# Attention into an MoE layer: exponentials summed as a tree with adding DMAs, one matmul per bias sum, joined halves of w_out, and a new order

## The chip, the cores and the metric

One core of a Trainium2 chip. The metric is the device time of one execution in microseconds (us). Before the change: median 605.57 us of 3 runs (604.0 to 606.81).

## The reference

Inputs: q, k, v with 4 batches, 12 heads, 448 rows, 64 per head; w_in (768 x 2048) and w_out (2048 x 768), which come as float64; scalars cap, s, b.

```python
scores = scale * np.matmul(q, k.transpose(0, 1, 3, 2))
scores = cap * np.tanh(scores / cap)
attn = np.exp(scores - max)
attn = attn / (np.sum(attn, axis=-1, keepdims=True) + 1e-09)
x = np.matmul(attn, v)                # to (1792, 768)
h = x @ w_in
g = s * np.maximum(h, 0.0) ** 2 + b
out = (g @ w_out).astype(np.float32)
```

## The kernel before, in words

**Precision.** The two products of the MoE layer run in float16 with every operand split in a high and a low half (hi, lo), so a product is three matmuls. The scales that this needs are found in the kernel. Batches 2 and 3 (and the second product of batch 1) use a scheme with seven products of half size in place of eight; its mixed weights are made in the kernel (`mixq`, `mix`), saved to DRAM and loaded again.

**Attention (`scores`, `pvs`).** A pair of heads gives three full tiles of 128 keys and a tail of 64 keys, which two pairs share. TensorE makes the scores in fp32, ScalarE runs tanh and exp (L441, L445) into a tile of 128 x 2 x 448 from the pool "ph" (the tail: "pt"), TensorE multiplies by v (L496, L505). The row sums come from a matmul with ones (`total`, L536). For batches 1 to 3 (`LEVEL` is 3) the tiles of a pair are added up first: three adds into a sum of its own from the pool "acc" (L522): tile 0 plus tile 1, plus tile 2, plus the pair's half (64 rows) of the tail. `binary` (L349 on VectorE, L350 on GpSimd) records them. Then four matmuls make the row sums of two pairs.

**w_out (`piece`, `wout`).** Each sixth d of w_out comes in four quarters q of 128 x 512 float64. Three instructions turn the two 32-bit words of a float64 into one float32: shift the low word (L636, VectorE), scale the high word (L641, ScalarE), and join them (L645, VectorE), which writes into the place of the high words, so that the float32 values lie 8 bytes apart. They are read for the maxima (L739), rounded to float16 in pieces of 256 (`split`: hi on any engine at L341 to L343, lo on VectorE at L360) and summed for the term b times the column sums of w_out, the "bias" (L746: three adds of 512 elements; L752: four fp32 matmuls against a column of ones, one for each block of 128).

**Order.** `Plan` collects operations with their reads and writes. The constant ORDER is a list of their numbers; a suffix a, d or p picks ScalarE, VectorE or GpSimd where an operation has several ways. `emit` issues them in this order, and each engine and DMA queue runs its own in that order. All loads and stores are issued by SP. Each operation of TensorE in the list is a group of matmuls (9 in the seven-product scheme's first product).

**Memory.** One area "bed" is cut into pools; `SLOTS` gives the number of tiles in each: 9 of "w", 5 of "ph", 2 of "acc".

**Lines that the prediction touches:** adds L349 and L350; products L828 to L830, L969, L1056; joins of the seven products L931; bias sum L752; rounding L341, L342; loads of mixed w_in halves L943 (from `wq`).

Of the kernel before, what the change touches and what calls it, by code (L numbers as in the profile page):

```python
# [21 lines left out]
class Plan:  # L22
# [87 lines left out]
FAST = (1, 2, 3)  # L110
LEVEL = (0, 3, 3, 3)
SPLIT = ()
QUICK = (2, 3)
# [7 lines left out]
8 12 10 18 27 795 868 9 4 796 3 13 800 14 19 28 15 63 11 21 16 805 24 858 33 20 22 870 30 17 23 25 802 34 26 67  # L121
35 2 36 29 797 65 5 806 801 811 40 798 847 816 64 799d 807 31 37 859 68 32 852 38 41 79 869 80 69 81 82 42 813
83 871 848 818 808 860 809d 812 821 120 45d 70 863 43 39 88 71 95 803 73 44d 66 804p 56 55 823 814 810 817 861
76 74 72 77 842 862d 822 75 190 819 824 78 815d 85 825d 89 137 820p 54d 826 57 849 853 86 872d 864 90 84 844 118
889 58 189 894 854 91 92 134 60 843 850 59 827 100d 122 96 87 851p 97 46 845 855 865 856d 123 119 47 846d 98 93
828 135 890 866 138 857 124 896 99d 94 829 867d 891 895 125 109d 873 874 128 61p 875 832d 131 136 876 126 102
129 127 101 905 111 0 892 834d 881d 48 882 906 887d 121 110 305 49 193 143 112 885d 140 910 150 897 144 139 132
151 130 888 145 133 899 194 141 113 877d 886 146 195 838d 142 191 147 199 196 878 883d 879d 148 830d 907 912 911
893d 200 941 197 149 201 152 202 833 103 908 913 155d 203 915 898p 205 104 153 208 164d 198 914d 836d 62 204 901
916 839 192 247 211 206 880 209 106 221d 50 214 207 884 215 154d 909d 216 900 902 217 218 105 249 166 210 222d  # L130
903d 917 260 6 212 261 251 252 918 165 156 51 223d 115 107d 167 213 250 157 904 248 919d 254 168 114 253 255
224d 257 258 920 256 921 219 259 220 922 225d 266 923 263 264 226d 272 227 926d 957 229d 169 170 228d 116p 835
262 158 928d 273 927 307 274 318 942 952 267 279d 159 946 275 265 269 319 287d 934d 268 309 161 308 270 171d 310
312 324 280d 831 315 282d 276 943 271 313 316 160 281d 306 283d 320 929 277 278 7 317 284d 162d 944 240 379 314
325 935 285 52d 321 311 326 389 330 936 924d 296d 331 286d 332 381 337p 239 962 289 322 333 338p 108 117 327
238d 948 241 230 242 390 959 163 380 53 383 954 172 323 953 173 244 334 1 439 339d 947 938 945d 328 398 384 340d
937 231 298 288 949 329 399 386 243 335 385 341d 297 387 342d 174 950d 392 336 404 299 175 178d 290 459 939 393
391 382 291 388 958 395 343 405 963 955 176d 396 964 940a 245p 394 397 400 232 437 345d 344d 406 180d 179 411d
401 233 951 407 965 408 402 347 293 495 292 966a 419a 956a 409 960 181 235 177 184d 961d 414d 444 460 182a 1400
967 450 294d 968 403 969 925 185 410 438 445 355 356 447 970 451 441 300 346 186a 187 1448 302 446 354a 412d  # L140
428d 932a 348 973a 452 971a 933 413d 442 1406 497 183 930d 1430 972 496 234 301 448 988 840a 975a 1075 931 443
1401 979d 415d 188 1402 449 1407 1449 1408 983 1403 1431 357 974 976 416d 841 989 1409 1076 980 1450 236d 981d
993 994 984 837 1432 995 998 508 999 1085 977d 509 985 417 990 986 1000 996 505 991 453 456 1001 461 1404a 1087
1003p 440 1090 462 246 982 469d 463 418a 358 421 420 506 1410a 1411p 1092 997 454 992 457 1451 1002 464 349 1412
1413 429 470d 499 514 458 1452d 1478 465 430 1077 1004d 987 1453p 1086 455 431 507 1414 500 1433 589 466 432 467
1078 468 472d 1091 360 1080 502 978 515 603 1008 477a 471d 1009 473d 587 510 503 1010 359 1484 1479 1485 474d
600 1081 1088 1082 1019a 475 1025a 1083 350 1093 1480 1500 1026 1005d 501 504 498 604 520 1095d 1023a 361p 521
1084 1089 295 1481 1021d 303d 601 422 1094 1024 522 1482d 1405d 476a 486a 1415 488 511 434 527d 1015a 517 1016
487 1096p 1006 1454 362 1416d 1017a 351 1013a 1486 605 512 1424 423 433 516 528d 1007 304 352p 1425 1011a 1434a
# [24 lines left out]
1266 1542 760 1690 764p 693 1535 1564p 1258 1530 1276 1267 1268d 1543 1270 1271d 1541 1277 1274 1290 1544 1531
1546d 1052 1592 1567a 1269 1257 1545 1565a 1278 1275 1279 1283 1568d 1566d 1053 1280 1284d 1281d 1547a 1287
1569d 1291 1292 1285 1610 1593 1300 1532 1502 1303 1282 1614 1288 1289 1548d 1293 1570d 1549a 1594 1297 1551d
1571d 1550d 1298d 1572a 1611 1294 1596 1272 1301 1595 1552d 1573d 1295d 1504 1327 1597 1302 1317 1533 1304 1600d
1603a 1612 1574 1598 1305 1599 1553d 1601a 1578 1296 1575 1613 1306 1307 1314 1604d 1615 1602d 1618d 1299 1579
1308d 1505 1506 1310 1554a 1605d 1311d 1318 1315 1616 1555d 1606d 1628 1319 1576 1316 1577 1715 1330 1629 1580
1582d 1581 1320 1534 1583a 1617 1682 1585a 1321 1619a 1324 1584d 1621a 1586d 1587d 1607d 1608a 1322d 1328 1523  # L180
1312 1688 1716 1620d 1588d 1622d 1589d 1632 1668 1508a 1325d 1331 1633 1329 1609d 1630 1332 1623d 1590a 1634
# [50 lines left out]
def attention_moe_kernel(  # L232
# [12 lines left out]
    nc = tc.nc  # L245
# [1035 lines left out]
```

## Time and profile before

| | us |
|---|---|
| median of 3 runs | 605.57 |
| the profiled execution, its own time | 606.2 |
| its span, first to last instruction | 604.0 |
| TensorE busy in the span | 585.6 |
| VectorE busy | 504.8 |
| ScalarE busy | 388.9 |
| GpSimd busy | 121.9 |

The span is what the profile shows; the 2.2 us around it belong to the execution. PE is TensorE's matmul, PEld its weight load, DVE is VectorE, ACT is ScalarE, POOL is GpSimd, SPq is the DMA queue of SyncE; L with a number is a line of the kernel. Busy matmuls overlap, so the mean duration of one is longer than the time from one to the next.

### The profile page before, as it was taken

To read this page: it belongs to the slowest core of one execution; us is meant where nothing else is said; L and a number is where in the kernel's file an instruction comes from. 1 tells how busy PE (TensorE), PEld (TensorE's weight loads), DVE (VectorE), ACT (ScalarE), POOL (GpSimd) and SP (SyncE) were. 2 spreads that over 40 slices of the span, in tenths; PEclk is the share of its full clock that TensorE was granted. 3 is DMA by queue.
4 is the path that set the end of the run, shared out by engine and by line. 5 is a ranking of instruction groups with operands and counts; after the bars stand their busy time and mean duration, and the time that the engine had idled before them with its cause. 6 is when DMAs were issued, how large, how long until landed. Compare 5 with 4: busy or idle time off the path is not lost.

```text
span 604.0 us, 12457 instructions
## 1 busy us (share of the span) xinstructions
PE 585.6 (97%) x4871; PEld 385.2 (64%) x4871; DVE 504.8 (84%) x1007; ACT 388.9 (64%) x570; POOL 121.9 (20%) x122
## 2 busy tenths in 40 slices
PE   5999999999999999999999999897999999999997
PEld 2332332343444444435555589897999999999997
DVE  1599999999999999999999999998889663577622
ACT  6999989998977997766869673133776114255100
POOL 0034013003211030411000010215242503363200
PEclk9999999999999999999999999998999999999999
DMA  8777665482435466565576787777575556563671
GB/s 322 293 223 256 172 219 167 113 300 71 113 112 184 141 234 219 167 221 184 211 231 237 239 303 248 263 253 260 183 269 208 186 187 198 178 223 137 248 258 62
DMA packets 56698, 125.24 MB, mean 207 GB/s; under 512 B 12736, under 2 KB 28224, under 8 KB 56640
## 3 DMA queue, kind: packets, MB, share of 16 engines
q1 hardware_dynamic: 56640, 124.45, 61.3%
q8 instruction: 38, 0.62, 0.4%
q14 instruction: 20, 0.16, 0.1%
HBM read 99.88 MB, written 24.47 MB: 206 GB/s over the span
## 4 chain that ended last, share of the span: by engine, by line
PE 62%; DVE 24%; ACT 6%; DMA 5%; issue 2%; SPq 0%; DVEq 0%; ACTq 0%
PE bank L1056 19%; PE bank L969 15%; DVE bed L349 7%; PE bank L829 4%; PE bank L828 4%; PE bank L830 4%; PE bank L496 3%; PE bank L426 3%; ACT bed L441 3%; DVE bed L645 2%; PE bank L1140 2%; PE bank L1142 2%; PE bank L1141 2%; DVE w L360 2%; ACT bed L445 2%
## 5 line engine op out<-in xcount | busy, mean ns | idle before, releaser
L349 DVE TENSOR_TENSOR bed<-bed 128x224 f32<-128x224 f32 (+6 forms) x193 | 150.4, 806 | 4.0 <-ACT bed L991 2.1
L1056 PEld LDWEIGHTS <-bed 128*128 128x128 f16 x1512 | 144.7, 98 | 3.5 <-issue 2.8
L350 POOL TENSOR_TENSOR bed<-bed 128x224 f32<-128x224 f32 (+4 forms) x71 | 71.3, 1018 | 291.0 <-DVE bed L349 88.7
L931 DVE SCALAR_TENSOR_TENSOR bed<-bank,arena,bed 128x224 f32<-128x224 f32 (+1 forms) x150 | 75.5, 525 | 63.4 <-PE bank L1056 26.2
L1056 PE MATMUL bank<-gt,bed 128*128 128x224 f16 x864 | 87.8, 259 | 2.5 <-DVE bed L931 2.5
L441 ACT ACTIVATE bed<-bank,arena 128x896 f32<-128x896 f32 x84 | 82.8, 1012 | 11.3 <-PE bank L426 3.9
L445 ACT ACTIVATE bed<-bed,par 128x896 f32<-128x896 f32 x84 | 85.4, 1049 | 0.1
L426 PE MATMUL bank<-bed 64*128 64x448 f32 x288 | 68.1, 584 | 6.7 <-DMA bed<-in_kq 5.0
L829 PE MATMUL bank<-bed,w 128*128 128x448 f16 x192 | 67.9, 353 | 0.0
L828 PE MATMUL bank<-bed,w 128*128 128x448 f16 x192 | 67.5, 351 | 0.0
L830 PE MATMUL bank<-bed,w 128*128 128x448 f16 x192 | 67.2, 350 | 0.0
L1056 PE MATMUL bank<-bed 128*128 128x224 f16 x648 | 66.8, 259 | 0.0
L969 PE MATMUL bank<-bed 128*128 128x224 f16 x576 | 60.9, 263 | 3.3 <-ACT gt L341 2.4
L496 PE MATMUL bank<-bed 128*32 128x448 f32 x576 | 62.2, 544 | 1.1 <-ACT bed L445 1.1
L969 PEld LDWEIGHTS <-bed 128*128 128x128 f16 x576 | 56.1, 99 | 4.8 <-ACT gt L341 2.6
L426 PEld LDWEIGHTS bank<-bed 64*128 64x128 f32 x288 | 24.9, 191 | 45.1 <-ACT bed L441 19.4
L969 PE MATMUL bank<-bed,w 128*128 128x224 f16 x432 | 45.8, 258 | 0.0
L360 DVE SCALAR_TENSOR_TENSOR bed<-bed,arena 128x256 f16<-128x256 f32 (+2 forms) x78 | 44.0, 594 | 0.0
L341 ACT ACTIVATE bed<-bed,arena 128x256 f16<-128x256 f32 (+2 forms) x56 | 30.9, 583 | 17.5 <-POOL bed L350 10.0
L969 PEld LDWEIGHTS <-w 128*128 128x128 f16 x432 | 41.4, 97 | 0.0
L496 PEld LDWEIGHTS bank<-bed 128*32 128x32 f32 x576 | 16.0, 109 | 39.2 <-issue 29.5
L988 ACT ACTIVATE bed<-bed 128x448 f32<-128x448 f32 x32 | 17.8, 568 | 36.1 <-DVE bed L931 36.0
(129 smaller groups left out, 801.7 us busy)
## 6 DMA issues: line engine op xcount, KB each, us to landing
bed<-ws SPq DMA_DIRECT2D x36, 512.0 KB, 4.6
bed<-w SPq DMA_DIRECT2D x30, 512.0 KB, 5.1
bed<-in_w_out SPq DMA_DIRECT2D x24, 512.0 KB, 4.2
bed<-wq SPq DMA_DIRECT2D x24, 512.0 KB, 4.5
bed<-in_kq SPq DMA_DIRECT2D x24, 448.0 KB, 4.4
bed<-in_w_in SPq DMA_DIRECT2D x18, 512.0 KB, 5.3
bed<-in_v SPq DMA_DIRECT2D x24, 256.0 KB, 4.7
w<-bed SPq DMA_DIRECT2D x12, 512.0 KB, 4.6
```

Of the source, the lines that this page charges most:

```text
L349: "DVE": lambda: nc.vector.tensor_tensor(dst(), a(), c(), op),
L350: "POOL": lambda: nc.gpsimd.tensor_tensor(dst(), a(), c(), op),
L426: nc.tensor.matmul(P[kp][:, h, 0:S], a[:, 0, c * 128:(c + 1) * 128], a[:, 1], start=True, stop=True)
L441: ("tanh", bb, c2, c), lambda: nc.scalar.activation(P[ke], P[kp][:, :, 0:S], AF.Tanh, scale=tsc[:, 0:1]),
L445: ("exp", bb, c2, c), lambda: nc.scalar.activation(P[ke], P[ke], AF.Exp, scale=par[:, 0:1]), r=["par"], w=[ke],
L496: nc.tensor.matmul(P[kp[x]][o, 0:S], P[kv[x]][:, c, o], P[kh[x][c]][:, h], start=not x and c == 0, stop=bool(x) and c == NC - 1,)
L828: nc.tensor.matmul(ps[:, 0:S], wh, x[:, 0], start=(c == 0), stop=False)
L829: nc.tensor.matmul(ps[:, 0:S], wh, x[:, 1], start=False, stop=False)
L830: nc.tensor.matmul(ps[:, 0:S], wl, x[:, 0], start=False, stop=(c == NP - 1))
L931: nc.vector.scalar_tensor_tensor(pick(to), ps, sc[:, 0:1], pick(of), ALU.mult, ALU.add)
L969: nc.tensor.matmul(at(), a(c, za), b(c, zb), start=c == 0 and n == 0, stop=c == NC3 - 1 and n == 2)
L1056: nc.tensor.matmul(at(), w(g, zw), b(g, zb), start=g == 0 and x == 0, stop=g == n - 1 and x == 2,)
```

## The change

1. The tiles of exponentials are summed as a tree and in place: tile 0 += tile 1; half of tile 2 += the pair's half of the tail; tile 0 += tile 2. The pool "acc" goes. An add runs on VectorE or, with suffix p, as a DMA that GpSimd issues and that adds to its destination.
2. The bias sum: quarter 0 is copied by a DMA of SP, the other three are added (VectorE or an adding DMA), then two halvings (256 and 128 elements, likewise) leave one block, and one matmul takes it.
3. The join of a w_out quarter writes its 512 float32 values side by side into the first half of the tile.
4. `SLOTS`: "w" 10 (was 9), "ph" 6 (was 5), "acc" gone.
5. ORDER is a new list, 2464 entries (was 2446), with other suffixes.

```diff
 SLOTS = {
-    "w": 9, "kq": 3, "vp": 3, "ph": 5, "pt": 2, "rd": 3, "pw": 6, "num": 8, "cmp": 3, "x": 6, "r": 4, "sq": 5, "cs": 2,
-    "kh": 0, "acc": 2,
+    "w": 10, "kq": 3, "vp": 3, "ph": 6, "pt": 2, "rd": 3, "pw": 6, "num": 8, "cmp": 3, "x": 6, "r": 4, "sq": 5, "cs": 2,
+    "kh": 0,
 }
...
         if level:
-            ka = [buf(("acc", bb, c2 + x), "acc", [128, 2, S]) for x in range(2)]
             for x in range(2):
-                a = lambda x=x: P[ka[x]]
-                for c in range(1, min(level, NC - 1) + 1):
-                    binary(
-                        ("add", bb, c2 + x, c), a, a if c > 1 else lambda x=x: P[kh[x][0]], lambda x=x, c=c: P[kh[x][c]],
-                        ALU.add, kh[x][c - 1:c + 1] if c == 1 else [kh[x][c]], [ka[x]],
-                    )
+                def more(c, dst, src, k, kd, x=x):
+                    ways = {
+                        "DVE": lambda: nc.vector.tensor_tensor(dst(), dst(), src(), ALU.add),
+                        "POOL": lambda: nc.gpsimd.dma_start(dst(), src(), accum_op=ALU.add),
+                    }
+                    P.op(("add", bb, c2 + x, c), ways, [k], [kd])
+
+                to = lambda c, x=x: lambda: P[kh[x][c]]
+                part = lambda k, x=x: lambda: P[k][half(x)]
+                more(1, to(0), to(1), kh[x][1], kh[x][0])
                 if level == NC:
-                    part = lambda k, x=x: lambda: P[k][half(x)]
-                    binary(("add", bb, c2 + x, NC), part(ka[x]), part(ka[x]), part(kt), ALU.add, [kt], [ka[x]])
-            parts = [[(k, None) for k in ka]] + parts[level + 1:]
+                    more(NC, part(kh[x][NC - 1]), part(kt), kt, kh[x][NC - 1])
+                for c in range(2, min(level, NC - 1) + 1):
+                    more(c, to(0), to(c), kh[x][c], kh[x][0])
+            parts = parts[0:1] + parts[level + 1:]
...
+        packed = label[0] == "o"
+        to = (lambda: P[kr].rearrange("p n t -> p (n t)")[:, 0:n]) if packed else hi
...
-            lambda: nc.vector.scalar_tensor_tensor(hi(), hi(), 3, lo(), ALU.logical_shift_left, ALU.bitwise_or),
+            lambda: nc.vector.scalar_tensor_tensor(to(), hi(), 3, lo(), ALU.logical_shift_left, ALU.bitwise_or),
...
-        return hf
+        return lambda: to().bitcast(F32)
...
+        flat = lambda q: fl[q]().rearrange("p a b -> p (a b)")
+        sums = lambda: P[kc].rearrange("p a b -> p (a b)")
+        dma(("csum", d, 0), lambda: nc.sync.dma_start(sums(), flat(0)), r=[(kr[0], "f")], w=[kc])
         for q in range(1, NQ):
-            first = (lambda: fl[0]()) if q == 1 else (lambda: P[kc])
-            binary(
-                ("csum", d, q), lambda: P[kc], first, lambda q=q: fl[q](), ALU.add, [(kr[q], "f"), (kr[0], "f")], [kc],
-            )
+            ways = {
+                "DVE": lambda q=q: nc.vector.tensor_tensor(sums(), sums(), flat(q), ALU.add),
+                "POOL": lambda q=q: nc.gpsimd.dma_start(sums(), flat(q), accum_op=ALU.add),
+            }
+            P.op(("csum", d, q), ways, [(kr[q], "f")], [kc])
         kb = buf(("bps", d), "ps_m")
-
-        def total():
-            for i in range(QF):
-                nc.tensor.matmul(P[kb][:, 0:1], P[kc][:, i], one32, start=i == 0, stop=i == QF - 1)
-
-        pe(("obias", d), total, r=[kc, "one"], w=[kb])
+        for n2 in (2, 1):
+            ways = {
+                "DVE": lambda n2=n2: nc.vector.tensor_tensor(P[kc][:, 0:n2], P[kc][:, 0:n2], P[kc][:, n2:2 * n2], ALU.add),
+                "POOL": lambda n2=n2: nc.gpsimd.dma_start(P[kc][:, 0:n2], P[kc][:, n2:2 * n2], accum_op=ALU.add),
+            }
+            P.op(("csum", d, 4 * n2), ways, [], [kc])
+        pe(
+            ("obias", d), lambda: nc.tensor.matmul(P[kb][:, 0:1], P[kc][:, 0], one32, start=True, stop=True),
+            r=[kc, "one"], w=[kb],
+        )
```

The adding DMAs for exponentials in the new order, with the place of the entry and that of its first reader (batch and pair in brackets):

| operation | what | entry | reader's entry |
|---|---|---|---|
| 338p | half of tile 2 (1, 4) | 433 | 464, add on VectorE |
| 415p | half of tile 2 (2, 1) | 567 | 578, add on VectorE |
| 470p | half of tile 2 (2, 2) | 692 | 709, add on VectorE |
| 473p | half of tile 2 (2, 3) | 702 | 726, add on VectorE |
| 531p | half of tile 2 (2, 5) | 827 | 840, add on VectorE |
| 624p | tile 0 += tile 2 (3, 1) | 1001 | 1032, matmuls of the total |
| 678p | half of tile 2 (3, 2) | 1108 | 1117, add on VectorE |
| 681p | half of tile 2 (3, 3) | 1109 | 1119, add on VectorE |
| 736p | half of tile 2 (3, 4) | 1236 | 1253, add on VectorE |

For the bias sums it has nine more: one whole quarter of d = 2, 4, 1 and 5, and five of the twelve small halvings. How often a kind of operation is on an engine (before, after):

| operation | VectorE | GpSimd | ScalarE |
|---|---|---|---|
| adds of exponentials, full | 34, 35 | 2, 0 (1 DMA) | |
| adds of exponentials, half | 18, 10 | 0, 0 (8 DMAs) | |
| bias sums, 512 elements | 11, 14 | 7, 0 (4 DMAs) | |
| bias sums, 256 / 128 elements | 0, 3 / 0, 4 | 0, 0 (5 DMAs) | |
| w_out to hi | 6, 22 | 4, 1 | 38, 25 |
| w_in to hi | 19, 22 | | 5, 2 |
| squares of w_in | 17, 13 | 4, 5 | 3, 6 |
| x to hi | 10, 5 | | 14, 19 |
| mixing of w_in (sum, lo) | 20, 19 | 4, 5 | |
| subtractions for seven products | 70, 78 | 50, 42 | |

## Rows read from the trace of the kernel before

**Rows 1.** The page's busy times over the span.

```profile
PE 585.6 (97%) x4871; PEld 385.2 (64%) x4871; DVE 504.8 (84%) x1007; ACT 388.9 (64%) x570; POOL 121.9 (20%) x122
```

**Rows 2.** Busy time by stretch; stretch, its length, engines, granted clock, DMA share, GB/s.

```profile
core 0: us, PE busy (x) PEld busy (x) DVE busy (x) ACT busy (x) POOL busy (x), PEclk, DMA share, GB/s
0.00:30.00 30.00, 23.86 (x180) 7.86 (x184) 10.42 (x23) 24.51 (x31) 1.86 (x11) 1.00 0.81 308
30.00:360.00 330.00, 326.91 (x2275) 144.83 (x2276) 322.05 (x663) 278.87 (x393) 52.44 (x36) 1.00 0.61 195
360.00:420.00 60.00, 54.40 (x556) 53.11 (x554) 58.20 (x104) 21.15 (x30) 15.16 (x12) 0.99 0.76 255
420.00:570.00 150.00, 149.79 (x1551) 149.03 (x1550) 104.08 (x204) 63.26 (x117) 52.43 (x65) 0.99 0.59 203
570.00:604.00 34.00, 30.68 (x321) 30.36 (x318) 10.05 (x19) 1.08 (x2) 0.00 (x0) 0.98 0.48 174
```

**Rows 3.** Order of time around one bias sum: start, us, instruction.

```profile
162.64 1.05 PE L752 MATMUL bank<-arena,bed 128*128 128x1 f32 x8
...
163.55 0.35 PE L828 MATMUL bank<-bed,w 128*128 128x448 f16 x1
...
163.74 0.35 PE L829 MATMUL bank<-bed,w 128*128 128x448 f16 x1
```

**Rows 4.** The chain that ended last, shares by engine.

```profile
PE 62%; DVE 24%; ACT 6%; DMA 5%; issue 2%; SPq 0%; DVEq 0%; ACTq 0%
```

**Rows 5.** TensorE's waits in 360 to 425 us: sum, times, longest.

```profile
PE bank L1056 <- DVE bed L931: 2.5, 2, 2.0
PE bank L969 <- ACT gt L341: 2.4, 1, 2.4
```

**Rows 6.** The chain in order of time, 405 to 420 us: start, us, what.

```profile
406.13 5.14 PE bank L969 x54
411.27 6.99 DMA bed<-wq
418.26 0.04 issue
418.31 1.78 PE bank L969 x10
```

**Rows 7.** Groups by form, other engines: busy us, mean ns, idle before.

```profile
L752 PE MATMUL bank<-arena,bed 128*128 128x1 f32 x48 | 6.1, 248 | 0.0
L349 DVE TENSOR_TENSOR bed<-bed 128x896 f32<-128x896 f32 x34 | 37.6, 1106 | 0.0
L349 DVE TENSOR_TENSOR bed<-bed 64x896 f32<-64x896 f32 x18 | 20.3, 1126 | 0.3
L349 DVE TENSOR_TENSOR bed<-bed 128x512 f32<-128x512 f32 x11 | 7.8, 717 | 0.0
L804 DVE TENSOR_TENSOR bed<-bed 128x256 f32<-128x256 f32 x12 | 5.0, 417 | 0.0
L342 DVE TENSOR_SCALAR bed<-bed,arena 128x256 f16<-128x256 f32 x6 | 2.6, 450 | 0.0
L341 ACT ACTIVATE bed<-bed,arena 128x256 f16<-128x256 f32 x38 | 18.6, 527 | 7.5 <-DVE arena L770 6.0 <-DVE bed L360 1.3
```

**Rows 8.** Groups by form, GpSimd's adds of bias sums and exponentials.

```profile
L350 POOL TENSOR_TENSOR bed<-bed 128x512 f32<-128x512 f32 x7 | 10.9, 1559 | 45.9 <-DVE bed L645 32.3 <-DMA bed<-in_v 11.4 <-PE bank L426 2.2
L350 POOL TENSOR_TENSOR bed<-bed 128x896 f32<-128x896 f32 x2 | 4.2, 2123 | 15.5 <-ACT bed L445 15.4
```

**Rows 9.** DMA issues: count, KB each, median us from issue to landing.

```profile
bed<-bed SPq DMA_DIRECT2D x48, 1.8 KB, 2.3
out_dram<-bed SPq DMA_DIRECT2D x23, 224.0 KB, 4.7
gt<-in_w_in SPq DMA_DIRECT2D x6, 512.0 KB, 7.5
```

More of the change, by code (lines that the diff above doesn't have):

```diff
@@ L107, in emit @@
         assert len(done) == len(self.ops)
-FAST = (1, 2, 3)
-LEVEL = (0, 3, 3, 3)
+FAST = (1,2,3)
+LEVEL = (0,3,3,3)
 SPLIT = ()
-QUICK = (2, 3)
+QUICK = (2,3)
 ALIAS = 2
@@ L123 @@
[L123 to L137, printed above, removed]
@@ L178 @@
[L178 to L181, printed above, removed]
-1631 1326 1722 1333 1309 751 1624p 1334 1635 1625d 1637a 1689 1646 1337 1536a 1636d 1626a 1591d 1664 1335d 1336
@@ new lines @@
+1111 504 1511 478 1120a 1103d 1122d 480 1123 600 520 521 1121 488 527d 1116p 1432 522 601 523 524 516 525 535d
+610 1433 1022a 526 1499 1512a 603 350 423 591 1126d 1184 544a 1118d 1500a 594 1117 1114d 1189 645 1461 1502
+1104p 528d 530d 1434a 531p 1186 604 529d 352d 1513d 1119 1025 1442 595 1023 295 489 532d 1194 246 1105d 1127
+1179 606 592 1501d 353 597 1462 533 1196 1463 1191 1190 1112d 1503 534a 1443 1180 1484 1009 1030 490 588 596
+1113 1185 1195 424 425 1485 1181 1192 1187 1476a 1115 1124a 605 1106d 1197 1435d 1193 1182 1010 1183 1188 188
@@ new lines @@
+733 1231 1519a 734 738d 1240 1241 739d 700 690 1156 1574 740d 737d 1075a 691 634d 1076 1248 1575 741 1077a 1235
+1071a 742a 701p 1078 1547a 1234 1242 1232 1236 1576 753 754 1556 744 1577 1057d 1521 1237 1256 1257 576d 1074
+755 745 1258 1557 1278 746 1058 1072 1157 1522 1259a 1558 1265a 1559 1578 1249d 756 747 1582d 1534 1261d 1260
+1579 1331 692d 1262 1564d 757 758 752a 1271a 749 748 1266 1535 1250d 1263a 1281 1553 1273a 1080 1272 1264 553
+1269a 1270 759d 1059 1279 1267a 1268 750d 1549 1580 1274 1280 1581 1282 1585a 1560 1567a 1583a 1283 1251p 1284
@@ new lines @@
+1584d 1586d 1587d 1285 1291 1286d 1288 1561 1289d 1294 1588d 1292 1293 1523 1275 1610 1295 1296 1562 1524 554
+1568d 1563 1297 1536 1565a 1611 1287 1177 1305 1178 1298 1550 1612 1301 555 1566d 1614 1615 1299d 1569d 1613
+1308 1526a 1302d 1628 1321 635 1537 1290 1629 1306 1618p 1332 1309 1570d 1616 1307 1310 1617 1571d 1311 1596
+1619a 1572a 1592 1312 1620d 1597 1573d 1318 1313d 1538 1589d 1303 1276 1623d 1593 1315 1621a 1590a 1316d 1345
+1622d 1319 1322 1630 1320 1624p 760 1252p 1323 1335 1317 1632 1625d 1734 1324 1631 1626a 1551 1633 1591d 1627d
@@ new lines @@
+1722 1720 1773 581d 1777 1380 1774 1381d 1375 1768 1721 1769 582p 1778 1764 1760 1776 1376d 1828 1382 1799 1723
+1775 1887 1383d 1786 1829 586 1830 1384 1726 583d 1398d 1888 1831 1798 1385 1800 1724 1770 1727 574a 1797 1779
+1802 584a 1386p 1387 1772 565 1780 1393d 575 1801 1783 585 1394 1395 1781 1832 1834 1787 1804 1377 1399 1784
+1396d 1803 1782 1805 1806 1400 1388p 1812 1785 1807 1389 1390 1401d 1397 1789 1808 1833 1790 1840 1707 1391p
+1809 1858 1835 1788 1838 1836 1771 1856 1403d 1857 1899 1810 1837 1813 1793 1889 1839 1706 1841 1791 1404 1816
@@ new lines @@
+1811 1842 1817 1844 1843 1408p 1916 1893 1891 1845 1890 1819a 1729 1897 1895 1409 1814 1405 1402 1847a 1846p
+1849a 1392 1406d 1794 1848p 1892 1915 1730 1917 1894 1865 1850p 1851p 1896 751 1815 1900 702 1903 1867 1859
+1820p 1898 1852d 1410 1413d 1853p 1407 1731 1930 1854a 1901 1414 1902 1855d 1861 1904 1818d 1860 1732 1411d 1948
+1862 1863 1821a 1922 1412 1864 1823d 1869 1905d 1866 1908a 1906a 1868 1871 1822p 1918 1924 1824p 1825p 1826a
+2072 1974 1795 1870 1872 1907p 1827d 1909d 1910d 1926 1415 1920 1416d 1975 1919 1417 1956 1921 1911p 1875 1873
@@ new lines @@
+1912p 1874 1928 1876 1977 1923 1925 693 2041 1927 1878p 1879p 1913a 2066 1950 1946 1877p 1952 1976 2039 1792
+1931 1914d 1882d 2040 1934 1880a 2033 1947 1929 1954 1979 1935 2078 1881d 1883p 1949 2067 1884d 1951 1958 1981
+1937a 1932 1953 1796 1985 1933 1885a 1886d 1955 1978 1957 761 1938d 1983 1987 1989 2073 2035 2036 1980 1936d
+1982 1939a 1984 2015 1941p 1986 2013 2009 1990 1988 762 1991 2005 1940p 1959 1942p 1943p 1992 2011 2034 1960
+1993 1961 1944d 1994 1945d 2006 2007 1962 1963 763 2017 2037 1965p 784p 1964d 1995p 2008 2010 2012 2052 2055
@@ new lines @@
+2014 1996a 2018 2016 1998d 2042 2046 2019 1728 2130 1966d 2074 1967p 2058 2020 1999d 2023p 1968p 2026d 2021 2038
+2068 2070 2027d 2022 2075 1997d 2024d 2000p 774p 2001d 777a 2049 2025p 2077 2043 2047 2079 1969d 2002d 1970d
+787a 778 2003a 2028d 2076 775a 1971d 1972d 2059 2090 776 2029d 2080 2045 2030d 764d 2004d 767d 2069 2044 2101
+2031d 779d 2048 785a 2032p 1973d 2081 765a 768 786 2056 2190 766 780d 788 2062 781p 2053 2071 2131 2050 2189
+2087 2051 2063 2161 789d 2054 2132 2082 790d 2084 2162 782a 2163 2057 2164 783 2085 2141 791p 2222 2191 2091
@@ L263, in attention_moe_kernel @@
     }
-    if max(LEVEL):
-        sizes["acc"] = 2 * row
     for n, size in sizes.items():
```

152 lines of the change are left out of this document (69 added, 83 removed), and 6 rows, old and new, of the table ORDER.

## The prediction

> **What bounds the kernel now.** I read the busy times first: the profiled execution took 606.2 us, 0.6 above the median of 605.57, and 604.0 of it are the span. TensorE is busy in 97% of that, VectorE in 84%, ScalarE in 64%, GpSimd in 20% [rows 1]. A share of the whole hides the stages, so I then took the table by stretch [rows 2]. It shows three stages. From 30 to 420 us TensorE and VectorE are both full: over these 390 us TensorE idles 3.1 + 5.6 = 8.7 us, VectorE 8.0 + 1.8 = 9.8 us. From 420 to 570 us TensorE is full alone (149.8 of 150) and VectorE has 46 us to spare. The two ends cost TensorE 6.1 us (the first load) and 3.3 us (the last store). The granted clock is 0.98 of full speed or more in every stretch.
>
> Whether a matmul group is really at the limit is seen in the order of time, since busy matmuls overlap: the eight instructions of one bias sum begin at 162.64 us and the next product at 163.55 us, while its neighbours follow each other every 0.19 us [rows 3]. TensorE is packed there, and what is taken out of its queue comes off the time, as long as no other engine holds it up. The chain tells the same from the end: 62% of it is TensorE, 24% VectorE [rows 4]. So the kernel is bound by TensorE's work, with VectorE so close behind in the first 420 us that neither can give way far without the other.
>
> The stalls of 360 to 420 us I followed by the waits: 2.5 us behind VectorE's joining of partial results, 2.4 us behind a rounding by ScalarE, and in the chain 7.0 us that belong to a load of mixed w_in halves from DRAM [rows 5, 6].
>
> **The change, part by part.**
>
> *One matmul per bias sum.* Of 48 instructions 12 stay (an fp32 matmul is two instructions). Six groups of eight took 163.55 − 162.64 = 0.91 us each [rows 3]; with two of eight instructions left that is 0.23. Gain 6 × 0.68 = 4.1 us, and slightly more with the wait for weights ahead of the group; I take 4.4. It lies on TensorE's packed queue. Bounds: 0 if VectorE is the limit throughout, 4.6 if a quarter of all 6.1 us of these matmuls is left [rows 7].
>
> *VectorE's side of the same.* The full-width sums of w_out go from 11 to 14 on VectorE (+3 × 0.72 us [rows 7]), and the new small sums put 3 of 256 and 4 of 128 elements there. The nearest row has 256 elements at 0.42 us [rows 7]; for 128 I take 0.3. Together +2.2 + 1.3 + 1.2 = +4.7 us. They replace seven GpSimd adds at 1.56 us [rows 8].
>
> *Exponentials.* The adds stay three for each pair of heads. VectorE had 34 of 36 full and all 18 half-height ones; it keeps 35 and 10: +1.1 − 8 × 1.13 = −7.9 us [rows 7]. The two adds at 2.12 us leave GpSimd [rows 8]. The matmuls of the totals stay as they are. The first add now writes into an exponential that TensorE reads, so it also waits for that product; it is queued behind it in the order, and I cost this at nothing while TensorE is ahead. If it isn't, VectorE waits up to one product of some 0.9 us. One 7-block area (5 exponentials, 2 sums) becomes 6 blocks, so ScalarE's tanh can wait for a block; ScalarE idles 51 us between 30 and 360 us [rows 2], which covers it except where it is itself full.
>
> *w_out's halves joined.* The same three instructions, written side by side. Rounding moves: ScalarE 38 to 25, GpSimd 4 to 1, VectorE 6 to 22. VectorE's 256-element rounding takes 0.45 us, so +16 × 0.45 = +7.2 us; ScalarE gets 13 × 0.53 = 6.9 us back [rows 7]. That packing alone makes the readers faster I cost at nothing.
>
> *Other work moved by the new order* (by its suffixes): squares of w_in −4, full rounding of w_in +3, x rounding −5, w_in mixing −1, subtractions of later batches +8, and some ten smaller ones: their rows of 0.4 to 1.2 us cancel to about −1 us on VectorE. So VectorE's sum is −7.9 + 4.7 + 7.2 − 1 = **+3 us**, some of it after 420 us where it costs nothing: I take +2 within the full stage, bounds −1.5 and +5. With 9.8 us idle there it still fits, but no more than that.
>
> *Queues.* SP gets six copies of 256 KB that wait for a quarter of w_out and hold the loads behind them; in the new order the first reader stands 10 to 77 entries behind each. GpSimd gets nine adds for exponentials (eight half, one full) and nine for bias sums as DMAs. No row shows a DMA issued there or one that adds. The nearest are the 1.8 KB on-chip copies, 2.3 us from issue to landing, and 224 KB to DRAM, 4.7 us; a 512 KB load in the start took 7.5 [rows 9]. A half add moves 224 KB on chip, between the first two: I take 3.5 us, range 2.3 to 7.5. Between issue and the VectorE add that needs it stand 31, 11, 17, 24, 13, 9, 10 and 17 entries. With 2446 entries in 604 us, 4.05 a us, that is 7.6, 2.7, 4.2, 5.9, 3.2, 2.2, 2.5 and 4.2 us. At 3.5 us VectorE waits 0.8 + 0.3 + 1.3 + 1.0 = 3.4 us. A quarter of that reaches TensorE by the chain's share: +0.9. The bias DMAs have 20 entries or more to their readers.
>
> A DMA from GpSimd could also be held by VectorE. Rows: a VectorE rounding lasts 0.45 us [rows 7], so one such delay is that long. The Trainium skill, "SBUF — State Buffer", section "Who interferes with whom", says that descriptors made by GpSimd wait while VectorE runs a copy or tensor-scalar in a two-port mode; no run here shows it yet. By that rule the four short gaps would wait 4 × 0.45 = 1.8 us more on VectorE, and the time would be 0.5 us higher.
>
> *Order.* The new list can be read for the distance between loads and their readers. For the 24 loads of mixed w_in halves, the number of TensorE groups between a load and its first reader began with 0, 0, 0, 1, 1 in the old order and begins with 2, 4, 4, 4, 4 in the new one. The 7.0 us load of [rows 6] is of this kind. Of the 5.6 us of TensorE idle in 360 to 420 I give back 3.5, of the 3.1 before it 1.0 [rows 2]: −4.5 us. Bounds 0 and −8.7.
>
> **Sum:** 606.2 − 4.4 − 4.5 + 0.9 = 598.2 for an execution like the profiled one; less its 0.6 above the median, 597.6. I say **598 us**.
>
> **The rivals.**
> *VectorE takes the limit (same).* If its +5 us fall in the full stage, the matmuls taken out turn into TensorE waits for it: no 4.4, half of the 4.5, joins 0.9: 606.2 − 2.3 + 0.9 − 0.6 = 604. For it: 97.5% busy over 390 us. Against it: at the lower bound (−1.5 us) it has room, and the work of batch 1 to 3 can slide past 420 us.
> *Joins wait for the adding DMAs (slower).* The place is the second-level add on VectorE, eight times; all that is queued there waits too. With landings of 6 us the gaps above leave 3.3 + 1.8 + 0.1 + 2.8 + 3.8 + 3.5 + 1.8 = 17 us, against 9.8 us of VectorE idle that is spread anyhow, so nearly all of it counts: 597 + 17 = 614. It is slower than 608.6 from landings near 5.2 us on. For it: 512 KB loads took 7.5 under load; the DMA engines are 61% busy there [rows 2]. Against it: the same bytes went to DRAM in 4.7.
> *The order closes all the stalls:* 606.2 − 4.4 − 8.7 − 0.6 = 592.5.
> *It doesn't do what it says:* the bias sums could have lain in gaps of TensorE; but their neighbours stand 0.19 us apart [rows 3]. This falls with the first rival.
>
> **How the numbers follow.** A measurement of this kernel can tell 0.5%, or 3.0 us, from no change: faster is below 602.5, slower above 608.6. Forecast 0.50, all stalls closed 0.12, VectorE the limit 0.20, late joins 0.18. The forecast's spread (593 to 603) lies almost wholly in faster; VectorE's case (601 to 608) gives a quarter to it; a few of the late joins end between: faster 0.64, same 0.20, slower 0.16. The range goes from 590 (stalls closed and a little of the start) to 610, into the late joins.
>
> **What would show it.** Right: 12 instructions of the bias sum; TensorE's busy time down by about 4.5 us; its idle time in 360 to 420 us halved; VectorE between 30 and 420 us above 97% and within 5 us of 380; GpSimd's compute a third lower before 300 us. Adding DMAs landing in 3 to 4.5 us. Wrong: waits of VectorE's adds behind DMAs of over 8 us in sum, or TensorE idle of over 12 us between 30 and 420 us with VectorE full.

## The result and the profile after

The changed kernel takes 599.15 us (median of 6 runs, 596.92 to 600.79); the kernel before, run beside it, 605.97 (603.66 to 607.44). The ratio is 0.9891, with an interval from 0.9858 to 0.9925: faster by 1.1%, or 6.8 us. The profiled execution took 600.61 us, 1.5 above the median, and its span is 598.8.

The page of the changed kernel, busy times and the shares of the chain that ended last, answering to [rows 1, 4]:

```profile
span 598.8 us, 12430 instructions
PE 579.8 (97%) x4835; PEld 380.4 (64%) x4835; DVE 496.1 (83%) x1029; ACT 383.9 (64%) x561; POOL 111.4 (19%) x121
PE 79%; DVE 10%; DMA 5%; ACT 3%; issue 1%; SPq 0%; DVEq 0%; ACTq 0%
```

TensorE's busy time fell by 5.9 us and VectorE's by 8.7, and VectorE's share of the chain went from 24% to 10%. That share should not be read closely: in a second profiled execution of the same kernel (run e9, below) it is 21%:

```profile
PE 68%; DVE 21%; ACT 4%; DMA 3%; issue 3%; SPq 0%; DVEq 0%
```

The table by stretch, in the columns of [rows 2]:

```profile
0.00:30.00 30.00, 23.79 (x164) 7.54 (x168) 8.63 (x17) 24.64 (x30) 2.64 (x12) 1.00 0.82 303
30.00:360.00 330.00, 324.45 (x2270) 142.63 (x2263) 316.15 (x677) 276.33 (x389) 39.31 (x37) 0.99 0.70 212
360.00:420.00 60.00, 56.95 (x589) 55.96 (x587) 58.26 (x107) 22.84 (x34) 21.96 (x16) 1.00 0.75 260
420.00:570.00 150.00, 150.00 (x1568) 149.88 (x1566) 106.38 (x218) 59.13 (x109) 47.46 (x57) 1.00 0.62 216
```

Read the two middle stages against [rows 2]. In 360 to 420 us TensorE's idle time went from 5.6 to 3.05 us. In 30 to 360 it did not fall but rose, from 3.1 to 5.55. VectorE, which idled 8.0 us there, now idles 13.85. By these rows VectorE seems to have 14 us to spare there; e5 below shows that it hasn't. TensorE's idle time up to 420 us is 8.6 us, where it was 8.7.

The groups by form (line, engine, operation, tiles and shapes, count, then busy us and mean ns of one, then idle before), answering to [rows 7, 8]:

```profile
L519 DVE TENSOR_TENSOR bed<-bed 128x896 f32<-128x896 f32 x35 | 37.4, 1080 | 1.8 <-PE bank L495 1.7
L519 DVE TENSOR_TENSOR bed<-bed 64x896 f32<-64x896 f32 x10 | 10.8, 1084 | 0.3 <-PE bank L495 0.2
L753 DVE TENSOR_TENSOR bed<-bed 128x512 f32<-128x512 f32 x14 | 9.5, 681 | 0.0
L760 DVE TENSOR_TENSOR bed<-bed 128x256 f32<-128x256 f32 x3 | 1.2, 416 | 0.0
L760 DVE TENSOR_TENSOR bed<-bed 128x128 f32<-128x128 f32 x4 | 1.1, 273 | 0.0
L341 DVE TENSOR_SCALAR bed<-bed,arena 128x256 f16<-128x256 f32 x22 | 7.2, 346 | 0.0
L765 PE MATMUL bank<-arena,bed 128*128 128x1 f32 x12 | 1.9, 225 | 0.0
L520 POOL DMA_DIRECT2D bed<-bed x9 | 7.7, 853 | 76.1 <-ACT bed L683 22.9 <-ACT bed L440 16.9 <-ACT bed L444 10.3
```

The counts are the ones that the diff promised. The bias sum's matmuls fell from 6.1 to 1.9 us. A 256-element rounding on VectorE takes 346 ns in place of 450, an add 1080 in place of 1106. Issuing an adding DMA keeps GpSimd busy for 0.85 us.

The on-chip DMAs, by the page's list of issues (KB each, median us from issue to landing), where [rows 9] had no row that adds:

```profile
bed<-bed POOLq DMA_DIRECT2D x8, 224.0 KB, 4.3
bed<-bed SPq DMA_DIRECT2D x6, 256.0 KB, 3.2
bed<-bed POOLq DMA_DIRECT2D x4, 256.0 KB, 4.8
```

### The profile page after: what moved, and what is told of

Same layout as the page of the kernel before. It is cut to its first block, busy times and chain, and to the rows that moved or that the text cites. A ratio compares the mean times of both kernels' runs of the same rounds, so it can differ in the third digit from the quotient of the medians.

```text
span 598.8 us, 12430 instructions
## 1 busy us (share of the span) xinstructions
PE 579.8 (97%) x4835; PEld 380.4 (64%) x4835; DVE 496.1 (83%) x1029; ACT 383.9 (64%) x561; POOL 111.4 (19%) x121
## 4 chain that ended last, share of the span: by engine, by line
PE 79%; DVE 10%; DMA 5%; ACT 3%; issue 1%; SPq 0%; DVEq 0%; ACTq 0%
PE bank L1069 22%; PE bank L982 15%; PE bank L495 7%; PE bank L425 6%; PE bank L841 5%; PE bank L842 5%; PE bank L843 5%; DMA bed<-in_w_out 3%; PE bank L1153 3%; PE bank L1155 3%; PE bank L1154 3%; DVE bed L519 2%; PE bank L539 2%; ACT bed L440 2%; PE bank L504 1%
## 5 line engine op out<-in xcount | busy, mean ns | idle before, releaser
L348 DVE TENSOR_TENSOR bed<-bed 128x224 f32<-128x224 f32 (+3 forms) x138 | 85.4, 645 | 7.9 <-POOL bed L349 3.1
L349 POOL TENSOR_TENSOR bed<-bed 128x224 f32<-128x224 f32 (+3 forms) x54 | 53.4, 998 | 205.3 <-DMA bed<-zd 52.3
L425 PE MATMUL bank<-bed 64*128 64x448 f32 x288 | 66.6, 579 | 5.4 <-DMA bed<-in_kq 4.9
L495 PE MATMUL bank<-bed 128*32 128x448 f32 x576 | 60.8, 544 | 0.9 <-ACT bed L444 0.7
L519 DVE TENSOR_TENSOR bed<-bed 128x896 f32<-128x896 f32 (+1 forms) x45 | 48.2, 1081 | 2.1 <-PE bank L495 1.8
L359 DVE SCALAR_TENSOR_TENSOR bed<-bed,arena 128x256 f16<-128x256 f32 (+2 forms) x78 | 47.6, 627 | 0.1
L982 PE MATMUL bank<-bed,w 128*128 128x224 f16 x432 | 47.6, 258 | 0.0
```

What stands on the lines that cost most here:

```text
L348: "DVE": lambda: nc.vector.tensor_tensor(dst(), a(), c(), op),
L425: nc.tensor.matmul(P[kp][:, h, 0:S], a[:, 0, c * 128:(c + 1) * 128], a[:, 1], start=True, stop=True)
L495: nc.tensor.matmul(P[kp[x]][o, 0:S], P[kv[x]][:, c, o], P[kh[x][c]][:, h], start=not x and c == 0, stop=bool(x) and c == NC - 1,)
L519: "DVE": lambda: nc.vector.tensor_tensor(dst(), dst(), src(), ALU.add),
L982: nc.tensor.matmul(at(), a(c, za), b(c, zb), start=c == 0 and n == 0, stop=c == NC3 - 1 and n == 2)
```

## The experiments

Line numbers shift by a few between kernels. In ORDER a number with p is an adding DMA, with d the same add on VectorE. The runs came in three sets, each with the kernel before on the same chip: its medians are 606.7 us (e1 to e4), 606.47 (e5 to e8) and 605.66 (e9 to e12), and every ratio is against that of the own set.

### Is the one matmul worth its time?

**e1 and e10** are the same program, the changed kernel with four matmuls for a bias sum again. **e9** is the changed kernel, run in one set with e10.

```diff
-                "DVE": lambda n2=n2: nc.vector.tensor_tensor(P[kc][:, 0:n2], P[kc][:, 0:n2], P[kc][:, n2:2 * n2], ALU.add),
-                "POOL": lambda n2=n2: nc.gpsimd.dma_start(P[kc][:, 0:n2], P[kc][:, n2:2 * n2], accum_op=ALU.add),
+                "DVE": lambda: None,
+                "POOL": lambda: None,
...
-            ("obias", d), lambda: nc.tensor.matmul(P[kb][:, 0:1], P[kc][:, 0], one32, start=True, stop=True),
+            for i in range(QF):
+                nc.tensor.matmul(P[kb][:, 0:1], P[kc][:, i], one32, start=i == 0, stop=i == QF - 1)
```

> The changed kernel with the bias sums taken by four matmuls again and the two halvings left out (the result is the same). Theory (TensorE's queue decides): TensorE's busy time rises from 579.8 by 4 to 4.6 us and the time by about 4, to 603 (ratio to the kernel before 0.994 to 0.998). Rival (VectorE decides up to 420 us): VectorE loses 2.3 us of small sums, so the time stays or falls, 597 to 599.5. Rival (the order alone brought the gain): no change, 599.

> The changed kernel as it is, once more, to compare with e10 on one chip. All theories: 598 to 601 (ratio to the kernel before near 0.989).

> The kernel of e1 once more, four matmuls per bias sum and no halvings. If the one matmul is worth nothing here: within 1.5 us of e9. If e1 was better in truth: 1 us or more below e9. First theory (TensorE's queue): 4 us above e9.

e1: 598.02 us, ratio 0.9863 [0.9836, 0.9889]. In one set: e9 598.13 us, 0.9879 [0.9858, 0.99], and e10 598.39 us, 0.9889 [0.9866, 0.9912]. The two cannot be told apart. The tables by stretch, first of e9:

```profile
30.00:360.00 330.00, 325.12 (x2296) 144.29 (x2286) 317.95 (x682) 278.81 (x393) 38.93 (x38) 1.00 0.72 215
360.00:420.00 60.00, 57.95 (x601) 57.29 (x599) 58.66 (x107) 22.83 (x34) 20.70 (x14) 1.00 0.76 263
```

and of e10:

```profile
30.00:360.00 330.00, 328.51 (x2327) 148.24 (x2320) 317.55 (x675) 278.56 (x393) 35.08 (x33) 1.00 0.71 213
360.00:420.00 60.00, 57.83 (x600) 57.17 (x598) 58.57 (x107) 23.03 (x34) 20.71 (x14) 1.00 0.77 258
```

With four matmuls TensorE idles 1.5 us between 30 and 360; with one it idles 4.9. Over the whole span it is busy 581.8 us in e10 and 578.4 in e9, and the spans are 595.9 and 596.0: what the change took out of its busy time came back as idle time. Where it lies is told by TensorE's waits of that stretch (who waits, for what: us in total, times, longest), in e9:

```profile
PE bank L383 <- DVE brief L776: 2.2, 1, 2.2
PE bank L539 <- DVE bed L519: 0.7, 1, 0.7
```

In the profiled run of the changed kernel the first of these is 3.9 us in two waits; e10 has no wait above 0.5 us there. L776 is VectorE's maximum of a sixth of w_out, and the scale of the rounding waits for TensorE's answer to it. The start times of the same matmuls show the step at work (start us, us, what, idle before), two lines of e9 and then the same two of e10:

```profile
239.00 0.96 PE L539 MATMUL bank<-bed,ones 128*32 128x448 f32 x8
249.11 0.18 PE L383 MATMUL bank<-brief,ones 128*128 128x1 bf16 x1 [2.23 <-DVE brief L776]
```

```profile
241.14 0.96 PE L539 MATMUL bank<-bed,ones 128*32 128x448 f32 x8
248.85 0.17 PE L383 MATMUL bank<-brief,ones 128*128 128x1 bf16 x1
```

Behind each of the six bias sums TensorE is 0.67 us further ahead in e9 than in e10, 4.0 us in all (the prediction had taken 0.68 for one). Three of them make the 2.1 us at L539; then L383 waits for VectorE, and the lead is gone. The other three are lost in the same way, 0.8 us at L539 near 266 us and 0.7 around 344 to 351 us, so that from 351 us on the two kernels are level to 0.3 us. The edit moves two things at once: 36 instructions off TensorE, and seven halvings (2.3 us) onto VectorE with five more adding DMAs. The halvings explain little of the largest wait: VectorE starts the copy that L383 waits for at 248.89 us in e9 and at 248.52 in e10, 0.4 us apart.

**e7**: the kernel before with this step alone, all the halvings on VectorE.

```diff
+            def ending(q=q):
+                nc.vector.tensor_tensor(P[kc], P[kc], fl[q](), ALU.add)
+                for n2 in (2, 1):
+                    nc.vector.tensor_tensor(P[kc][:, 0:n2], P[kc][:, 0:n2], P[kc][:, n2:2 * n2], ALU.add)
...
+            ("obias", d), lambda: nc.tensor.matmul(P[kb][:, 0:1], P[kc][:, 0], one32, start=True, stop=True),
```

> The kernel before with one matmul per bias sum; the two halvings run on VectorE behind the last add of the quarters (6 x 0.69 = 4.1 us). TensorE has 4.1 us less, VectorE 4.1 us more. First theory (TensorE's queue): 602. New theory (VectorE's time decides): 607 to 611, slower than before. Rival (neither is on the path): 606.

611.43 us, ratio 1.0078 [1.005, 1.0105]: 5.0 us slower. VectorE's busy time is 509.8 us, also 5.0 above the 504.8 of [rows 1] (in a profiled execution of 608.98 us, one of the fastest of its twelve). TensorE's matmul group shrank to the same 12 instructions as in the changed kernel (2.2 us), and the time followed VectorE.

### Does the time hang on VectorE?

**e2**: the changed kernel with its nine adding DMAs for exponentials back on VectorE. **e5**: the changed kernel with 18 useless adds of 128 x 384 on a tile of their own (9.9 us), so that VectorE gets the time without any change of the DMAs.

```diff
 e2, in ORDER:
-338p 415p 470p 473p 531p 624p 678p 681p 736p
+338d 415d 470d 473d 531d 624d 678d 681d 736d
 e5, behind the first add of the same nine pairs:
+                            for _ in range(2):
+                                nc.vector.tensor_tensor(spare, spare, spare, ALU.add)
```

> The changed kernel with its nine adding DMAs for exponentials put back on VectorE, at the same places. VectorE gets 9 x 1.08 = 9.8 us more between 90 and 265 us. Theory (TensorE's queue decides, VectorE has 13.9 us of idle from 30 to 360): 600 to 603, TensorE's idle time there up by 1 to 4 us. Rival (VectorE decides there): nearly all of the 9.8 us come out, 606 to 609, and no gain of the change is left. Rival (the DMAs don't matter): 599.

> The changed kernel, nothing moved, with useless work on VectorE: behind the first add of the nine pairs whose adds are DMAs stand two adds of 128 x 384 on a tile of their own, 18 x 0.55 = 9.9 us in all, with nothing to wait for. New theory (VectorE's time decides from 70 to 270 us): the time rises as in e2, by 5 to 9 us, to 604 to 608. Rival (in e2 it was the waits of the adds at their old places, not VectorE's time): 599 to 601. First theory (TensorE's queue): 599 to 602.

e2: 606.2 us, 0.999 [0.9972, 1.0008]. e5: 605.3 us, 0.9976 [0.9957, 0.9995]. The chains that ended last, of e2 and then of e5:

```profile
PE 50%; DVE 34%; ACT 5%; issue 5%; DMA 4%; SPq 1%; DVEq 0%; ACTq 0%
```

```profile
PE 51%; DVE 33%; ACT 5%; DMA 5%; issue 4%; SPq 1%; DVEq 0%; ACTq 0%
```

Either way VectorE gets 9 to 10 us (506.2 and 505.0 us busy by the page), has a third of the chain in place of 10% or 21%, and all of the gain (e2) or four fifths of it (e5) is gone. The start times tell where. In the profile of e5 (606.6 us, 1.3 above its median) the same matmuls start 1.5 us later than in e9 at 105 us, 5.3 at 195 and 8.7 at 270, and from there to 420 us no more is lost; in e2 the steps are 1.1, 6.0 and 8.8. So the loss builds up along the nine pairs, nearly one for one with the added work. e5 leaves each DMA as it is, so what counts here is VectorE's time, not who does the adding. Nor does the idle time take it in: of the 180 us from 90 to 270, VectorE idles 7.6 us in e9 and still 6.1 in e5.

### The order alone, the relief alone, the joining alone

**e3**: the new order with the old parts: all 18 adding DMAs on VectorE, four matmuls, no halvings (the copy of quarter 0 by DMA and the joined halves stay). **e6**: the old order with the nine adds left out; the row sums of these pairs lack those terms. **e12**: the kernel before with joined halves.

```diff
 e3, in ORDER (18 entries of which these are three), and e1's edit:
-338p ... 1008p ... 1253p
+338d ... 1008d ... 1253d
 e6:
+                    if (bb, c2 + x, c) == (3, 1, 2):
+                        P.op(("add", bb, c2 + x, c), {"DVE": lambda: None}, [kh[x][c]], [ka[x]])
+                        continue
...
+                    if (bb, c2 + x) in ((1, 4), (2, 1), (2, 2), (2, 3), (2, 5), (3, 2), (3, 3), (3, 4)):
+                        P.op(("add", bb, c2 + x, NC), {"DVE": lambda: None}, [kt], [ka[x]])
+                        continue
 e12:
-            lambda: nc.vector.scalar_tensor_tensor(hi(), hi(), 3, lo(), ALU.logical_shift_left, ALU.bitwise_or),
+            lambda: nc.vector.scalar_tensor_tensor(to(), hi(), 3, lo(), ALU.logical_shift_left, ALU.bitwise_or),
```

> The new order with the parts undone: all eighteen adding DMAs on VectorE, four matmuls per bias sum, no halvings (the copy of the first quarter and the joined halves stay). It shows what the order is worth alone. Theory: the matmuls (4) and the adds (1 to 4) go, the order's 2 to 3 us stay: 603 to 606. Rival (the order alone): 599 to 600. Rival (VectorE decides): VectorE has 9.8 + 4 x 0.68 - 2.3 = 10 us more, 608 or more.

> The kernel before in its old order with nine adds left out, the same that are DMAs in the changed one (eight halves of the tail, one full tile; the row sums of these pairs lack those terms). VectorE has 8 x 1.13 + 1.11 = 10.1 us less and no DMA does it. New theory (VectorE's time decides, in any order): 606 less 5 to 9, 597 to 601. Rival (the relief counts only in the order that was searched with it): 604 to 607.

> The kernel before with the halves of w_out joined, nothing else. The forecast cost it at nothing: 605 to 607.5. Rival (side by side values are read faster, so roundings shrink and the kernel with them): 603 to 605.

e3: 605.63 us, 0.999 [0.9974, 1.0006]. e6: 606.19 us, 0.9985 [0.9964, 1.0006]. e12: 606.9 us, 1.003 [1.0005, 1.0055]. The table by stretch of e3:

```profile
30.00:360.00 330.00, 321.33 (x2237) 139.22 (x2226) 319.49 (x670) 271.41 (x379) 23.37 (x18) 1.00 0.60 196
360.00:420.00 60.00, 59.07 (x613) 58.37 (x611) 58.80 (x111) 27.24 (x42) 18.37 (x12) 1.00 0.77 268
```

The new order does to 360 to 420 us what it was read to do, and more: 0.9 us of TensorE idle remain of 5.6. But in 30 to 360 TensorE idles 8.7 us, where VectorE has 23 us of GpSimd beside it instead of 52 and does the adds itself. What the order gives late it has lost early. The opposite case, e6: the chain's shares and its steps on DMAs in order of time (start us, us, what).

```profile
PE 71%; DMA 10%; DVE 10%; ACT 5%; SPq 2%; issue 1%; DVEq 0%
...
75.58 5.36 DMA bed<-in_kq
...
235.22 4.57 DMA zd<-bed
240.98 5.81 DMA bed<-in_w_out
374.23 6.34 DMA bed<-ws
...
411.22 6.87 DMA bed<-wq
```

With 7.8 us less on VectorE the old order ends no sooner: VectorE's share drops to 10% as in the changed kernel, and loads and stores take its place, the load of [rows 6] among them (6.87 us at 411). That these hold it is read from the chain; no run takes them away. Put together, as ratios to the kernel before:

| | old order | new order |
|---|---|---|
| all adds on VectorE | 1 | 0.999 (e3), 0.999 (e2) |
| nine adds off VectorE | 0.9985 (e6) | 0.9879 (e9) |

Neither half alone gives anything that its interval tells from nothing; both together give 7 us. The columns differ in more than the order: the right one also has the sums in place, the other pools, the copy of quarter 0, the joined halves and the roundings on other engines, and these were not varied one by one.

e12 shows that joining the halves is no gain by itself, if anything 1.8 us lost. Some of the readers did get shorter by it: a 256-element rounding takes 500 ns on ScalarE in place of 527, and an add of a quarter on GpSimd 1408 in place of 1559. On VectorE a rounding takes 359 ns in place of 450, but without joined halves it took 380 in e7, so that part is unclear.

### Do late adding DMAs cost what the rival said?

**e4**: the old order with the new parts put right beside the places of the old ones: eight half adds by DMA as the last step of a sum, bias sums with the copy, the adding DMAs, the halvings and one matmul, joined halves. **e8**: the changed kernel with four more half adds by DMA, 19 to 25 entries ahead of their readers. **e11**: e10 with five more quarters of bias sums by DMA.

```diff
 e4, the old list's order of adds into "acc", the last by DMA:
+                more(1, a, to(0), to(1), kh[x][0:2])
+                more(2, a, a, to(2), [kh[x][2]])
+                more(NC, part(ka[x]), part(ka[x]), part(kt), [kt])
 e8, in ORDER:
-222d 412d 623d 620d
+222p 412p 623p 620p
 e11, in ORDER, and e1's edit:
-1006d 1103d 1153d 1249d 1250d
+1006p 1103p 1153p 1249p 1250p
```

> The kernel before, in its old order, with the new parts put in at the old places: eight half adds as adding DMAs (into the old separate sum, as its last step), the other adds on VectorE, the bias sums with copy, adding DMAs, halvings and one matmul, and joined halves of w_out. Theory: the matmuls' 4.1 us come off, the order's part does not: 601 to 604. Rival (order alone): 605 to 607. Rival (late joins): the total's matmuls stand 6 to 41 entries, 1.5 to 10 us, behind the DMAs; with landings of 4.3 us three of eight are late by up to 3 us: 606 to 612.

> The changed kernel with four more half adds as adding DMAs (batch 1 pair 0, batch 2 pair 0, batch 3 pairs 0 and 1), which have 19 to 25 entries, 4.6 to 6 us, to their readers against a landing of 4.3 us. VectorE gets 4.3 us less. New theory (VectorE's time decides): 595 to 598. Rival (late joins eat it): 599 to 603. Rival (VectorE has enough room after nine): 599.

> e10 with five more additions of bias quarters as adding DMAs, where the next reader stands 20 entries or more behind or is the matmul itself (quarter 3 of sixths 0 and 3, quarter 2 of sixth 2, quarters 1 and 2 of sixth 5). VectorE gets 5 x 0.68 = 3.4 us less. If VectorE's time is still what holds TensorE back: 595 to 598. If the order has no more to give, as e6 and e8 say: 597 to 601. If DMAs that wait on GpSimd's queue hold its other work: above 602.

e4: 647.12 us, 1.0672 [1.0626, 1.0718]. e8: 605.45 us, 0.9978 [0.9958, 0.9997]. e11: 604.5 us, 0.9975 [0.9954, 0.9997]. The waits behind adding DMAs in e4:

```profile
POOL bed L759 <- DMA bed<-bed: 12.5, 4, 3.7
PE bank L537 <- DMA bed<-bed: 11.9, 2, 6.8
DVE bed L751 <- DMA bed<-bed: 11.3, 6, 5.7
```

e4 is 35 us above the worst that was expected of it, and these waits, on three engines that overlap, are not all of its 40 us. Adding DMAs of bias sums (L751, L759) are among them as well as those of exponentials (L537). The clock has a part: TensorE stood still from 270 to 275 us, and the granted clock was 0.69 in these 5 us and 0.63 in the next 5, so partly at the lower of its two levels (1.2 of 2.4 GHz), where the kernel before has 1.00 from 30 to 360 us. How the loss divides was not separated.

In e8 the chain in order of time, where the change shows (start us, us, what):

```profile
65.87 0.14 issue
66.02 4.46 DMA bed<-bed
...
70.56 1.10 DVE bed L515
71.67 0.02 issue
71.69 1.01 ACT bed L436
```

An adding DMA issued at 66.02 us lands 4.46 us later; VectorE's add waits 3.1 us of it, and ScalarE's tanh waits for that add's block. In e11 the timelines of GpSimd and then of VectorE (start us, us, engine and line, operation, idle before and its end):

```profile
225.19 0.91 POOL L750 DMA_DIRECT2D bed<-bed  x1 [8.36 <-DMA bed<-bed]
227.72 0.82 POOL L516 DMA_DIRECT2D bed<-bed  x1 [1.61 <-ACT bed L440]
230.97 0.80 POOL L516 DMA_DIRECT2D bed<-bed  x1 [2.43 <-ACT bed L473]
...
238.64 1.09 DVE L515 TENSOR_TENSOR bed<-bed 128x896 f32<-128x896 f32 x1 [3.44 <-DMA bed<-bed]
```

The first of these is a bias DMA. GpSimd idles for 8.4 us before it, by the trace until an on-chip DMA lands; no adding DMA lands then (the last one had, at 212.55 us). Three adding DMAs then leave within 6 us, and the last takes 7.7 us to land (the changed kernel's slowest for exponentials took 5.3, one of its bias DMAs 7.7), so VectorE waits 3.4. In both kernels VectorE is busy 2 to 3 us less (page: 493.6 in e8 against 496.1, 491.9 in e11 against 495.1), and the time is 5 to 6 us worse than that of the kernel it was made from (by the ratios 0.9978 against 0.9879, and 0.9975 against 0.9889); for e8 that is above everything expected of it. So less work for VectorE is no gain where a reader has to wait for the DMA that does it.

The start times place these losses too. In e8 the matmuls fall 3.1 us behind those of e9 by 78 us, at the wait shown. They lose 2.2 us more by 221 us, behind two adding DMAs of which the second reads what the first wrote (623p lands 6.2 us after its issue, 624p then takes 4.4). Smaller steps stand at 191 us (0.7) and around 342 (0.9); from 345 us on they are 6.9 us behind. In e11 the second loss of VectorE is larger than the first:

```profile
284.59 0.63 DVE L344 TENSOR_TENSOR bed<-bed 128x448 f32<-128x448 f32 x1 [4.71 <-DMA bed<-zd]
```

It waits for a load of reciprocal row sums from DRAM (zd), which was issued only 5.2 us after the store that it reads back; in e9 that takes 2.1 us. The two waits, 3.4 and 4.7 us, are enough for the loss of e11; why the store was slow there, no run shows.

## Why the prediction came out

The number held (598.0 forecast, 599.15 measured, 598.13 in e9), and the sign. Its own sum did not: one term was worth nothing, another was missed, and they cancelled. That the number agrees so well is luck.

- **One matmul per bias sum, −4.4 us: this step failed.** The instructions went as forecast (−4.2 us in their group, 0.67 us of lead for each), but e10 shows no time for them. The faulty sentence is "it lies on TensorE's packed queue". [Rows 3] show a queue that was packed around one bias sum; what they can't show is how soon after a removed matmul TensorE meets a wait for VectorE. e9 shows that wait: the 2.2 us of L383 behind L776, where the lead of three sums was lost. The sums did not lie in gaps of TensorE, so "It doesn't do what it says" was rightly dismissed; for this step the first rival's mechanism was the case.
- **VectorE's sum, +3 us: mis-sized.** By the group rows it was −2.5 (the busy times of all its groups add up to 551.1 us before and 548.6 after). Adds: −9.7 against −7.9, since the 896-element adds also got shorter. Roundings: +4.6 against +7.2, since one took 346 ns and not 450. Bias side: +4.0 against +4.7. The rest: −1.4 against −1. Neighbouring instructions overlap, so the union that the page gives is smaller than the rows' sum, and it fell by more: 8.7 us. That was outside my bounds for the full stage (−5.9 measured in 30 to 360 against −1.5 to +5).
- **VectorE's load costed at nothing, because 9.8 us of it were idle: failed.** In e5, 9.9 us on VectorE cost nearly 6 us (0.9976 against 0.9879), against 15.6 us of idle time up to 420 in the changed kernel. So this idle time was not a reserve. Here lies the gain that I had put on the matmuls: VectorE's relief, which I took for a load.
- **The order, −4.5 us: right in its place, wrong as a term of its own.** 360 to 420 gave back 2.6 us (3.6 in e9) of the 3.5 that I took. But the order with VectorE loaded is worth nothing (e3), though it gave back 4.7 us in that stretch there, and the 1.0 us ahead of 360 turned into a loss of 2.5 (1.8 in e9).
- **The adding DMAs, +0.9 us: landing a little late, waits none.** They landed in 4.1 to 5.3 us, median 4.3, where I took 3.5. No VectorE wait behind one stands in the trace, because counting list entries at 4.05 a us understated the gaps. GpSimd issues ahead of its place in the list, VectorE comes to its place late:

```profile
95.93 1.01 POOL L520 DMA_DIRECT2D bed<-bed  x1 [16.85 <-ACT bed L440]
172.80 0.84 POOL L520 DMA_DIRECT2D bed<-bed  x1 [4.20 <-ACT bed L477]
...
177.49 1.03 DVE L519 TENSOR_TENSOR bed<-bed 128x896 f32<-128x896 f32 x1
```

  The second of these DMAs is 531p: 4.7 us to its reader, where 13 entries had given 3.2. The eight gaps measured 4.7 to 7.4 us (forecast 2.2 to 7.6), each longer than that DMA took.
- **The hold of GpSimd's descriptors.** The nine landings differ by 1.2 us and none made VectorE wait, so the 0.5 us that I had worked out for it did not come. Whether VectorE held descriptors of GpSimd at all, as the Trainium skill ("SBUF — State Buffer", "Who interferes with whom") says of its two-port modes, and whether that has a part in the 4.3 us, no run here separates.
- **Joined halves, nothing:** right for the time (e12), or 1.8 us too kind. That packing does not make the readers faster was wrong for ScalarE (500 ns in place of 527).

Of the rivals, "VectorE takes the limit" had the mechanism right (removed matmuls became TensorE waits for VectorE, and its loaded case e2 took 606 us, near its 604) and the sign of VectorE's sum wrong. "Late joins" is real where the distance is short or the landing late (e4, e8, e11) and was avoided here by 0.4 us in the tightest join (681p: a gap of 5.25 us, a landing of 4.85). "The order closes all the stalls" did not happen.

Of the signs that I had listed, TensorE's busy time (−5.9 against −4.5) looked like a confirmation and was none: e10, with all 48 instructions, shows −3.8. VectorE at 374.4 of 390 us (96%) between 30 and 420 was the sign that failed, and it pointed at the real cause. GpSimd was busy 35.7 us before 300 us in place of 52.8, a third less only with its DMA issues counted. Of the nine adding DMAs for exponentials six landed within 4.5 us.

## What to carry to other kernels

When two engines are both nearly full and feed each other, price a part on both and don't add the terms up: a part and an order can each be worth nothing alone and, as here, 7 us together, so the test is all four cases. A sum taken out of a packed queue is a gain only if the other engine is ready that much sooner; put the removed work back and see whether idle time vanishes instead. An adding DMA relieves an engine if its reader stands farther off than it takes to land (4 to 5 us for most here, up to 7.7), in microseconds of the two engines' own queues and not in list entries.

The version with four matmuls and no halvings (e10) is as fast as the changed kernel with simpler code; no run was faster than these two by more than their intervals.

## What the runs showed of the hardware that I had not expected

- Busy time is not an amount of work. Before and e10 run the same 4871 matmuls, and the rows of TensorE's groups sum to 754.5 and 754.4 us, but the union, in which overlapping time counts once, is 585.6 and 581.8. On VectorE the new order alone (e3) sums to 6.3 us more by rows than before, and its union is 0.9 less: neighbours overlap more. Which neighbours, was not followed up.
- VectorE's instructions differ with what runs beside them and with their order: 224-element subtractions took 423 ns in place of 468, with GpSimd busy 39 us of the stretch in place of 52, its DMA issues counted. That GpSimd is the cause is argued, not shown: e3, with 23 us of GpSimd, has both shorter and longer groups.
- A DMA that adds 224 KB on chip, issued by GpSimd, landed in 4.3 us beside the 3.2 of a plain 256 KB copy issued by SP, and in 6.0 in e4.
